# Normalizing three attention units right behind their softmax, and unread TensorE products in the opening rounds

## The chip, the cores and the metric

The kernel runs on one core of one Trainium2 chip. The time is device time in microseconds (us) of one execution, lower is better. Three runs gave 1222.81, 1223.53 and 1228.38 us; their median is 1223.53 us.

## The reference

Chunked attention over 4 x 8 heads and 768 positions, then two feed-forward blocks on its output, in float32:

```python
for c in range(nc):                       # chunks of 32 queries
    scores = scale * np.matmul(q_c, k_full.transpose(0, 1, 3, 2))   # 8 memory keys and up to 56 of context
    scores = scores - np.max(scores, axis=-1, keepdims=True)
    a = np.exp(scores)
    a = a / (np.sum(a, axis=-1, keepdims=True) + 1e-09)
    out[:, :, c_start:c_end] = np.matmul(a, v_full)
x = out.transpose(0, 2, 1, 3).reshape(B * S, H * D)                 # 3072 x 512
h = x @ w_in;  g = np.maximum(h, 0.0) + np.log1p(np.exp(-np.abs(h)));  x = g @ w_out
return (x @ w_a) * (x @ w_b) @ w_o2
```

## The kernel before

The 3072 rows of x are worked off in eight tiles of 384. Each large product is made of three float32r products of a high and a low part, so every weight matrix is split on the chip first. A `Weight` does that in two halves: `top` (ScalarE) and `value` (VectorE) first, then `high` (ScalarE) and `low` (VectorE).

Attention of the first tile goes through six `Block`s of 64 queries. They stand in rounds, a software pipeline written out by hand: round `i` normalizes block `i-2`, places block `i-4` into x, makes the scores of block `i`, transposes block `i-2` on TensorE (`pat`), multiplies with the values of block `i-3` (`pxb`), and converts one weight beside that. Ten rounds come before the first feed-forward product `ph0` of tile 0, which reads all of x of that tile.

Attention of later tiles goes through `Unit`s of 128 queries, laid between the products of the tile before. Tile 0 has 16 products `ph0` to `ph15` (`emit_h`), each followed on ScalarE by three activations `e` and a cast of `g` to its high part, on VectorE by `g` and its low part (`emit_soft`), and, two products later, by the second product (`emit_x1`, written `px`). In the same stretch the remaining 24 weights are converted, half by half (`convert`), and units 3, 4 and 5, which are the second tile, run through `EARLY_STEPS`: scores (`sc`), softmax (eight reductions on VectorE, eight exponentials on ScalarE), normalization on VectorE, eight transposes on TensorE (`pa`), copies of them (`af`), values (`pxa`), and a place into x.

In tile 0 the instructions of all five engines stand in the order in which the code issues them (a manual schedule), so each engine works through its own queue in that order and waits on semaphores for the others. Two PSUM banks carry the tag `att`: the two score banks of a unit, its two transposes and its values take them in turn, so that the second score bank of unit `u+1` is the bank of the values of unit `u` and is free when these have been placed. `acc`, with one bank a tag, holds the scores of a block, and `h`, with two, holds `ph`.

Of the kernel before, what the change touches and what calls it, by code (L numbers as in the profile page):

```python
# [9 lines left out]
F32 = mybir.dt.float32  # L10
# [11 lines left out]
         (3, "values"), (3.1, "place"))  # L22
START = 1.7
SETS = 1
EARLY_STEPS = (((4.9, "scores"), (5, "soft"), (6, "norm_v"), (9, "flip_p"), (10.9, "values"), (11, "place")),
               ((11.9, "scores"), (12, "soft"), (14, "norm_v"), (17, "flip_p"), (18.9, "values"), (19, "place")),
               ((19.9, "scores"), (20, "soft"), (22, "norm_v"), (25, "flip_p"), (26.9, "values"), (27, "place")))
EARLY = len(EARLY_STEPS)
NEXT_LATER = 1.5

# [2 lines left out]
EARLY_RAW = (2, 4, 5, 6, 7, 8)  # L33
PACKED_AT = (0, 0.1, 2, 2.1)
AHEAD = 6
ROUNDS_CV = 7
CV_DONE = 15
OUT_TAGS = "eegg"
# [7 lines left out]
def attn_moe_moe2(ctx: ExitStack, tc: tile.TileContext, q, k, v, mem_k, mem_v,  # L46
                  w_in, w_out, w_a, w_b, w_o2, out):
    nc = tc.nc
# [5 lines left out]
    P = 128  # L54
# [17 lines left out]
        name=nc.get_next_instruction_name(), act_func_set_id=6, ins=[], outs=[]))  # L72
# [8 lines left out]
    ps = ctx.enter_context(tc.tile_pool(name="ps", bufs=2, space=PSUM))  # L81
# [9 lines left out]
    def fetch(dst, key, src):  # L91

        u = n_w[0]
        n_w[0] += 1
        raw = wp.tile([P, 1024], U32, tag="w", name=f"raw{u}")
        nc.sync.dma_start(raw if len(src.shape) == 2 else raw.rearrange("p (a b) -> p a b", a=src.shape[1]),
                          src.bitcast(U32))
        dst[key] = u, raw
# [33 lines left out]
    def fetch1(n):  # L132
        dst, f = uses[n]
        if dst is w1:
            fetch(w1, f, w_in[:, f * P:(f + 1) * P].rearrange("(k p) f -> p k f", p=P))
        else:
            fetch(w1o, f, w_out[f * P:(f + 1) * P, :])

    masks = [ap.tile([P, KB], F32, name=f"mask{i}") for i in range(4)]
    ident = wp.tile([P, P], F32, tag="w", name="ident")  # L140
# [234 lines left out]
    def normalize(engine, sm, st):  # L375
        nc.vector.tensor_scalar(st[:, 2, :], st[:, 1, :], 1.0e-9, None, ALU.add)
        nc.vector.reciprocal(st[:, 3, :], st[:, 2, :])
        r = st[:, 3, :].rearrange("p (h o) -> p h o", o=1)
        engine.tensor_tensor(sm, sm, r.to_broadcast([P, sm.shape[1], KB]), ALU.mult)

    class Unit:
# [57 lines left out]
        def flip2(self):  # L439
            self.flip((2, 3))  # L440

        def norm_v(self):
            normalize(nc.vector, self.sm, self.st)

        def flip_p(self):
# [18 lines left out]
        def place(self):  # L464
# [3 lines left out]
            nc.scalar.copy(xh, self.px)  # L468
            nc.vector.tensor_tensor(xl, self.px, xh.bitcast(F32), ALU.subtract)  # L469

    blocks = [Block(u) for u in range(BPT)]
    units = [Unit(u) for u in range(B * NU)]

    plan = []
    for i, unit in enumerate(units[UPT:]):
        at = 2 * NF1 * (i + 1) // UPT - START + NEXT_LATER * (i == EARLY)
        steps = STEPS
        if i < EARLY:
            steps = EARLY_STEPS[i]
            at = steps[-1][0]  # L480
# [321 lines left out]
    def order():  # L802
# [6 lines left out]
        def fetch_to(n):  # L809
            nonlocal n_w1  # L810
            while n_w1 < min(n, len(uses)):
                fetch1(n_w1)
                n_w1 += 1
# [10 lines left out]
        packed[1].load(1)  # L824
        fetch_to(1 + ROUNDS_CV + AHEAD)
        weights = [Weight(*use) for use in uses]
# [4 lines left out]
            getattr(weights[0], step)()  # L831
        for i in range(BPT + 4):
            for d, step in ROUND:
                if d is None:
                    n = i if step == "low" else i + 1
                    if 0 < n <= ROUNDS_CV:
                        getattr(weights[n], step)()
                elif 0 <= i - d < BPT:
                    getattr(blocks[i - d], step)()

        rest = weights[1 + ROUNDS_CV:]
        firsts = [(w.top, w.value) for w in rest]
        seconds = [(w.high, w.low) for w in rest]
        halves = [firsts[0]]
        for x, y in zip(firsts[1:] + [()], seconds):
            halves += [x, y]
        n_half, n_point = [0], [0]

        def convert():

            n_point[0] += 1
            while n_half[0] * 3 * CV_DONE < n_point[0] * len(halves) and n_half[0] < len(halves):
                for step in halves[n_half[0]]:
                    step()
                n_half[0] += 1

        def att_at(slot):
            while plan and plan[-1][0] <= slot:
# [6 lines left out]
        for n, e in enumerate(pre[:n_pre]):  # L865
            t, i = divmod(n, PRE)
# [27 lines left out]
        for t in range(NTILE):  # L894
            if t == 1:
                early.close()
                early.enter_context(tc.manual_schedule(engines={mybir.EngineType.SP, engines["P"], engines["V"]}))
            if t == NTILE - 1:
                assert not plan
                actx.close()  # L900
                early.close()
                ctx.enter_context(tc.manual_schedule(engines={mybir.EngineType.SP, *engines.values()}))
                late["x"] = ctx.enter_context(tc.tile_pool(name="late", bufs=5))
            for f in range(NF1):
                ph = emit_h(t, f)
                if t == 0:
                    fetch_to(1 + ROUNDS_CV + AHEAD + len(rest) * (f + 1) // CV_DONE)
                    convert()
                    emit_soft(t, f, ph, nc.vector, convert)
                    convert()  # L910
                elif t < NTILE - 1:
                    emit_soft(t, f, ph)
                else:
                    emit_soft(t, f, ph, nc.vector, partial(slot, 2 * f), partial(slot, 2 * f + 1))
                att_at(2 * (NF1 * t + f))
                if len(pend) >= LAG:
                    emit_x1(*pend.pop(0))
                pend.append((t, f))
                att_at(2 * (NF1 * t + f) + 1)
# [48 lines left out]
        while jobs:  # L968
            if len(jobs) == 3 and pair_step.late:
                pair_step.late.pop()()  # L970
            next_job()

    order()


# [28 lines left out]
```

## Time and profile before

| | |
|---|---|
| median of three runs | 1223.53 us |
| profiled execution, its own time | 1221.9 us |
| its span in the trace | 1219.9 us |
| TensorE busy with matmuls | 1181.3 us (97%) |
| VectorE, ScalarE, GpSimd busy | 734.4, 537.8 and 277.9 us |
| mean granted TensorE clock | 0.986 of full |

The span runs from the first to the last instruction on the core. TensorE is called PE, its weight loads PEld, VectorE DVE, ScalarE ACT. [...] In the rows, "[2.84 <-DVE work L368]" means that the engine stood 2.84 us ahead of this instruction and that an instruction of line 368 on VectorE ended the wait.

### The profile page before, as it was taken

What the parts mean: (1) busy time and instruction counts of PE and PEld (TensorE: products, weight loads), DVE (VectorE), ACT (ScalarE), POOL (GpSimd) and SP (SyncE); (2) the same over time, 40 slices, a digit from 0 to 9 for tenths busy, and PEclk for the clock granted to TensorE, in tenths of its full rate; (3) what the DMA queues carried; (4) which work ended last, traced back from release to release, by engine and by line L of the source; (5) the groups of instructions that cost most, each with busy time, mean ns of one, the idle gap of its engine ahead of it and who ended that gap; (6) DMA issues with size and microseconds to landing.
All of it is one profiled execution on the core that took longest, in us unless ns stands there. A gap on an engine that the chain in (4) does not pass through costs nothing.

```text
span 1219.9 us, 21427 instructions
## 1 busy us (share of the span) xinstructions
PE 1181.3 (97%) x7920; PEld 1119.7 (92%) x7920; DVE 734.4 (60%) x1706; ACT 537.8 (44%) x1329; POOL 277.9 (23%) x249
## 2 busy tenths in 40 slices
PE   6888999999999999999999999999999999999998
PEld 6787999999989999999999999999999999999997
DVE  6778565555645546555357777764666456664565
ACT  5788755575655756556464433312012111212010
POOL 1000222233222222222242877500211002200000
PEclk7799999999999999999999999999999999999999
DMA  9943335344352343533164987679463975469521
GB/s 243 299 149 83 75 96 123 93 97 92 111 104 79 98 96 93 112 101 95 44 225 160 375 295 275 264 245 376 158 233 118 354 270 177 151 214 382 197 78 52
DMA packets 198696, 209.84 MB, mean 172 GB/s; under 512 B 121616, under 2 KB 149952, under 8 KB 198592
## 3 DMA queue, kind: packets, MB, share of 16 engines
q1 hardware_dynamic: 198208, 208.43, 53.6%
q8 instruction: 62, 1.02, 0.3%
q14 instruction: 42, 0.34, 0.1%
q0 software_dynamic: 384, 0.05, 0.0%
HBM read 158.11 MB, written 50.33 MB: 171 GB/s over the span
## 4 chain that ended last, share of the span: by engine, by line
PE 82%; DVE 5%; ACT 4%; SPq 4%; DMA 2%; issue 2%; DVEq 0%; ACTq 0%
PE ph L514 18%; PE py L724 16%; PE px L537 16%; PE pV L701 8%; PE pW L701 8%; PE pX L701 8%; PE pY L701 4%; SPq L176 1%; SPq L178 1%; ACT sm L372 1%; PE pxa L461 1%; PE sc L418 1%; DVE af L436 1%; ACT e L521 1%; ACT e L522 1%
## 5 line engine op out<-in xcount | busy, mean ns | idle before, releaser
L514 PE MATMUL ph<-x,w 128*128 128x384 f32 x1536 | 295.5, 340 | 9.0 <-DVE x L469 4.4
L514 PEld LDWEIGHTS ph<-x,w 128*128 128x128 f32 x1536 | 269.7, 190 | 13.7 <-DVE x L469 6.0
L724 PE MATMUL py<-w2o,c 128*128 128x512 f32 x864 | 223.1, 394 | 0.7 <-DVE c L794 0.5
L524 DVE SCALAR_TENSOR_TENSOR g<-ph,e 128x384 f32<-128x384 f32 x128 | 71.3, 557 | 222.9 <-ACT e L522 216.2
L724 PEld LDWEIGHTS py<-w2o,c 128*128 128x128 f32 x864 | 159.9, 188 | 27.0 <-DVE c L794 1.2
L783 ACT CAST c<-c 128x384 fp32r<-128x384 f32 x48 | 24.7, 514 | 303.9 <-DVE c L781 271.3
L701 PE MATMUL pX<-x,u 128*128 128x384 f32 x576 | 115.5, 334 | 0.0
L520 ACT ACTIVATE e<-ph 128x384 f32<-128x384 f32 x128 | 62.3, 487 | 118.9 <-PE ph L514 104.9
L733 DVE TENSOR_TENSOR y<-py,y 128x512 f32<-128x512 f32 x120 | 82.9, 691 | 48.6 <-PE py L724 48.1
L701 PEld LDWEIGHTS pX<-x,u 128*128 128x128 f32 x576 | 102.1, 188 | 4.1
L436 DVE STREAM_TRANSPOSE af<-sm 32x256 f32<-32x256 f32 x180 | 78.2, 434 | 2.5
L521 ACT ACTIVATE e<-e 128x384 f32<-128x384 f32 x128 | 67.3, 526 | 4.1
L522 ACT ACTIVATE e<-e 128x384 f32<-128x384 f32 x128 | 67.3, 526 | 3.9
L779 DVE TENSOR_TENSOR d<-pW,q 128x384 f32<-128x384 f32 x48 | 26.7, 557 | 68.3 <-PE pW L701 68.3
L372 ACT ACTIVATE sm<-sm,st 128x96 f32<-128x96 f32 x168 | 60.5, 362 | 7.5 <-DVE st L368 7.5
L793 ACT CAST c<-c 128x384 fp32r<-128x384 f32 x48 | 24.6, 513 | 78.1 <-DVE c L791 77.1
L701 PE MATMUL pW<-xs,u 128*128 128x384 f32 x288 | 57.8, 335 | 0.0
L701 PE MATMUL pV<-xx,u 128*128 128x384 f32 x288 | 57.8, 335 | 0.0
L701 PE MATMUL pV<-xs,u 128*128 128x384 f32 x288 | 57.6, 334 | 0.0
L701 PE MATMUL pW<-xx,u 128*128 128x384 f32 x288 | 57.6, 334 | 0.0
L701 PE MATMUL pY<-xs,u 128*128 128x384 f32 x288 | 57.6, 334 | 0.0
L701 PEld LDWEIGHTS pV<-xx,u 128*128 128x128 f32 x288 | 51.5, 188 | 4.1
(247 smaller groups left out, 2226.1 us busy)
## 6 DMA issues: line engine op xcount, KB each, us to landing
u<-u_scratch SPq DMA_DIRECT2D x108, 512.0 KB
u_scratch<-u SPq DMA_DIRECT2D x36, 512.0 KB
w2o<-w2o_scratch SPq DMA_DIRECT2D x36, 512.0 KB
u<-u_scratch SPq DMA_DIRECT2D x36, 256.0 KB
raw<-in_moe_w_in_dram SPq DMA_DIRECT2D x16, 512.0 KB
raw<-in_moe_w_out_dram SPq DMA_DIRECT2D x16, 512.0 KB
vn<-in_v_dram SPq DMA_DIRECT2D x35, 176.0 KB
raw_a<-in_moe_w_a_dram SPq DMA_DIRECT2D x12, 512.0 KB
```

Source lines behind the costliest of these rows:

```text
L372: nc.scalar.activation(sm[:, h], sm[:, h], AF.Exp, bias=st[:, 0, h:h + 1], scale=-1.0, accum_out=st[:, 1, h:h + 1])
L436: nc.vector.transpose(out=af[32 * kb:32 * kb + 32, x], in_=self.sm[32 * x:32 * x + 32, :, 32 * kb:32 * kb + 32])
L514: nc.tensor.matmul(ph, lhsT=a, rhs=c, start=n == 0, stop=n == 3 * KT - 1)
L520: nc.scalar.activation(e, ph, AF.Abs)
L521: nc.scalar.activation(e, e, AF.Exp, scale=-1.0)
L522: nc.scalar.activation(e, e, AF.Ln, bias=1.0)
L524: nc.vector.scalar_tensor_tensor(g, ph, 0.0, e, ALU.max, ALU.add)
L537: nc.tensor.matmul(acc[t][i][:, :TT], lhsT=a, rhs=c, start=f == 0 and m == 0, stop=f == NF1 - 1 and m == 2)
L701: nc.tensor.matmul(bank[:, :TT], lhsT=u[:, j, a, kt * P:kt * P + P], rhs=x[:, c, kt, :], start=first_ and m == 0, stop=m == 3 * KH - 1, sk ...
L724: nc.tensor.matmul(b, lhsT=c[:, x, r], rhs=w[:, y], start=n == 0, stop=n == 3 * GROUP - 1)
L733: tt(y, b, y, ALU.add)
L779: tt(d21, w[:, :TT], q, ALU.add)
```

## The change

Two things. First, for units 3, 4 and 5 the steps `soft` and `norm_v` become one step `weigh`: it takes the next half of a weight conversion from the common list, issues that half's ScalarE part, then the softmax, then the half's VectorE part, and at once the normalization on VectorE. The halves are taken from the same list, so as many are converted as before. Second, `FILL` names 16 places in the rounds, and `warm` issues there, 44 in all, products of the 128x128 identity with itself into a bank of tag `h` that nothing reads.

```diff
-EARLY_STEPS = (((4.9, "scores"), (5, "soft"), (6, "norm_v"), (9, "flip_p"), (10.9, "values"), (11, "place")),
-               ((11.9, "scores"), (12, "soft"), (14, "norm_v"), (17, "flip_p"), (18.9, "values"), (19, "place")),
-               ((19.9, "scores"), (20, "soft"), (22, "norm_v"), (25, "flip_p"), (26.9, "values"), (27, "place")))
+EARLY_STEPS = (((4.9, "scores"), (5, "weigh"), (9, "flip_p"), (10.9, "values"), (11, "place")),
+               ((11.9, "scores"), (12, "weigh"), (17, "flip_p"), (18.9, "values"), (19, "place")),
+               ((19.9, "scores"), (20, "weigh"), (25, "flip_p"), (26.9, "values"), (27, "place")))
...
+FILL = {(2, "scores"): 11, (2, "flip"): 14, (3, "flip"): 1, (3, "values"): 1, (4, "scores"): 2, (4, "flip"): 1,
+        (4, "values"): 1, (5, "scores"): 2, (5, "flip"): 1, (5, "values"): 1, (6, "flip"): 4, (6, "values"): 1,
+        (7, "flip"): 5, (7, "values"): 1, (8, "values"): 1, (9, "place"): 1}
...
+    halves, n_half = [], [0]
+
+    def next_half():
+        n_half[0] += 1
+        return halves[n_half[0] - 1]
...
-        def norm_v(self):
+        def weigh(self):
+            on_scalar, on_vector = next_half()
+            on_scalar()
+            self.soft()
+            on_vector()
             normalize(nc.vector, self.sm, self.st)
...
+    def warm(n):
+
+        if n:
+            n_fill[0] += 1
+            bank = ps.tile([P, 512], F32, tag="h", name=f"fill{n_fill[0]}")
+            for _ in range(n):
+                nc.tensor.matmul(bank[:, :P], lhsT=ident, rhs=ident, start=True, stop=True)
...
         for i in range(BPT + 4):
             for d, step in ROUND:
+                warm(FILL.get((i, step), 0))
```

On VectorE, behind the reductions of unit 3's softmax, the queue before (`w12` is the low half of a weight, `g0_3` the result for `ph3`, `tmp14` and `tmp15` first halves of weights, `st3` and `sm3` the sums and the weights of unit 3):

```order
L125 TENSOR_TENSOR w12_878<-tmp12_773,w12_878 128x512
L524 SCALAR_TENSOR_TENSOR g0_3_885<-ph0_3_861,e0_3_881 128x384
L116 TENSOR_SCALAR tmp14_888<-raw14_617 128x512
L117 SCALAR_TENSOR_TENSOR tmp14_888<-raw14_617,tmp14_888 128x512
L504 TENSOR_TENSOR g0_3l_892<-g0_3_885,g0_3h_891 128x384
L125 TENSOR_TENSOR w13_895<-tmp13_790,w13_895 128x512
L116 TENSOR_SCALAR tmp15_899<-raw15_693 128x512
L117 SCALAR_TENSOR_TENSOR tmp15_899<-raw15_693,tmp15_899 128x512
L376 TENSOR_SCALAR st3_844<-st3_844 128x8
L377 RECIPROCAL st3_844<-st3_844 128x8
L379 TENSOR_TENSOR sm3_843<-sm3_843,st3_844 128x768
L125 TENSOR_TENSOR w14_934<-tmp14_888,w14_934 128x512
```

The same place on VectorE in the changed kernel:

```order
L128 TENSOR_TENSOR w12_907<-tmp12_837,w12_907 128x512
L385 TENSOR_SCALAR st3_910<-st3_910 128x8
L386 RECIPROCAL st3_910<-st3_910 128x8
L388 TENSOR_TENSOR sm3_909<-sm3_909,st3_910 128x768
L546 SCALAR_TENSOR_TENSOR g0_3_952<-ph0_3_931,e0_3_948 128x384
L119 TENSOR_SCALAR tmp14_955<-raw14_681 128x512
L120 SCALAR_TENSOR_TENSOR tmp14_955<-raw14_681,tmp14_955 128x512
L526 TENSOR_TENSOR g0_3l_959<-g0_3_952,g0_3h_958 128x384
L128 TENSOR_TENSOR w13_962<-tmp13_854,w13_962 128x512
L119 TENSOR_SCALAR tmp15_966<-raw15_757 128x512
L120 SCALAR_TENSOR_TENSOR tmp15_966<-raw15_757,tmp15_966 128x512
L128 TENSOR_TENSOR w14_998<-tmp14_955,w14_998 128x512
```

The three instructions of the normalization have moved up past seven others, ahead of `g0_3`. On ScalarE at the same place, before (`raw13` is the first half of a weight, `sm3` the eight exponentials, `w12` the high half, `e0_3` the first activation for `ph3`):

```order
L111 ACTIVATE raw13_199<-raw13_199 128x512
L372 ACTIVATE sm3_843,st3_844<-sm3_843,st3_844 128x96 x8
L122 CAST w12_878<-tmp12_773 128x512
L520 ACTIVATE e0_3_881<-ph0_3_861 128x384
L521 ACTIVATE e0_3_881<-e0_3_881 128x384
```

And in the changed kernel:

```order
L114 ACTIVATE raw13_199<-raw13_199 128x512
L125 CAST w12_907<-tmp12_837 128x512
L381 ACTIVATE sm3_909,st3_910<-sm3_909,st3_910 128x96 x8
L542 ACTIVATE e0_3_948<-ph0_3_931 128x384
L543 ACTIVATE e0_3_948<-e0_3_948 128x384
```

The cast of `w12` now stands ahead of the exponentials. Units 4 and 5 are moved likewise; there the half is `raw20` and `w25`. On TensorE the last rounds and the first product read like this before (`pat4`, `pat5` transposes of blocks, `pxb` their values):

```order
L352 MATMUL pxb2_522<-afb2_469,vv2_159 64x64 x8
L344 MATMUL pat4_552<-ident_75,work4_439 96x128 x4
L352 MATMUL pxb3_558<-afb3_515,vv2_159 64x64 x8
L344 MATMUL pat5_576<-ident_75,work5_493 96x128 x4
L352 MATMUL pxb4_582<-afb4_551,vv4_168 64x64 x8
L352 MATMUL pxb5_593<-afb5_575,vv4_168 64x64 x8
L514 MATMUL ph0_0_604<-x0_435,w0_277 128x384 x12
```

And in the changed kernel:

```order
L361 MATMUL pxb2_567<-afb2_505,vv2_159 64x64 x8
L490 MATMUL fill11_596<-ident_75 128x128 x4
L353 MATMUL pat4_602<-ident_75,work4_473 96x128 x4
L490 MATMUL fill12_608<-ident_75 128x128
L361 MATMUL pxb3_610<-afb3_558,vv2_159 64x64 x8
L490 MATMUL fill13_627<-ident_75 128x128 x5
L353 MATMUL pat5_634<-ident_75,work5_534 96x128 x4
L490 MATMUL fill14_640<-ident_75 128x128
L361 MATMUL pxb4_642<-afb4_601,vv4_168 64x64 x8
L490 MATMUL fill15_653<-ident_75 128x128
L361 MATMUL pxb5_655<-afb5_633,vv4_168 64x64 x8
L490 MATMUL fill16_664<-ident_75 128x128
```

Nothing is moved on TensorE; the fills stand between. The largest, of 11 and 14, stand ahead of the scores of block 2 and of the transposes of block 0.

## Rows read from the trace of the kernel before

**Rows 1.** Windows: busy us (instructions) by engine, granted clock, DMA share, GB/s.
```profile
17.30:34.30 17.00, 13.87 (x160) 12.07 (x160) 14.81 (x68) 14.53 (x50) 0.00 (x0) 0.50 0.94 238
34.40:37.70 3.30, 1.67 (x32) 1.27 (x32) 3.06 (x14) 3.07 (x12) 0.00 (x0) 1.00 1.07 255
37.80:48.00 10.20, 7.28 (x58) 6.31 (x53) 6.46 (x16) 4.94 (x15) 0.00 (x0) 0.50 1.06 372
48.00:135.00 87.00, 78.45 (x758) 74.90 (x757) 65.50 (x163) 71.10 (x170) 0.00 (x0) 1.00 0.50 139
362.10:368.80 6.70, 6.10 (x19) 6.10 (x20) 1.02 (x2) 1.54 (x3) 0.00 (x0) 0.50 0.39 94
```
**Rows 2.** Timeline of TensorE in the rounds: start, us, instruction, [idle before].
```profile
18.29 0.56 PE L293 MATMUL scb<-kt,qt 64*64 64x88 f32 x4 [2.84 <-DVE work L368]
...
22.51 1.06 PE L344 MATMUL pat<-ident,work 128*96 128x128 f32 x4 [2.02 <-ACT raw L111]
...
40.65 1.06 PE L344 MATMUL pat<-ident,work 128*96 128x128 f32 x4 [2.45 <-ACT x L358]
41.64 1.98 PE L352 MATMUL pxb<-afb,vv 96*64 96x64 f32 x32
44.09 4.22 PE L514 MATMUL ph<-x,w 128*128 128x384 f32 x12 [0.47 <-ACT x L358]
```
**Rows 3.** Timeline of VectorE and ScalarE where the rounds end.
```profile
39.95 0.56 DVE L379 TENSOR_TENSOR work<-work 128x384 f32<-128x384 f32 x1
...
43.66 0.37 ACT L358 CAST x<-pxb 128x256 fp32r<-128x256 f32 x1 [0.48 <-PE pxb L352]
44.06 0.42 DVE L359 TENSOR_TENSOR x<-pxb,x 128x256 fp32r<-128x256 f32 x1 [0.43 <-ACT x L358]
```
**Rows 4.** Timeline of TensorE in tile 0, around the units.
```profile
73.88 1.05 PE L450 MATMUL pa<-ident,sm 128*96 128x128 f32 x8 [3.37 <-DVE sm L379]
74.69 2.36 PE L514 MATMUL ph<-x,w 128*128 128x384 f32 x12
...
82.42 0.40 PE L293 MATMUL sc<-kn,qn 64*64 64x88 f32 x8
...
97.17 1.05 PE L450 MATMUL pa<-ident,sm 128*96 128x128 f32 x8 [2.82 <-DVE sm L379]
...
120.37 1.05 PE L450 MATMUL pa<-ident,sm 128*96 128x128 f32 x8 [2.34 <-ACT raw L111]
```
**Rows 5.** Timeline of ScalarE around the exponentials of units 3 and 4.
```profile
63.37 0.38 ACT L372 ACTIVATE sm<-sm,st 128x96 f32<-128x96 f32 x1 [1.34 <-DVE st L368]
...
66.26 0.60 ACT L122 CAST w<-tmp 128x512 fp32r<-128x512 f32 x1
66.77 0.48 ACT L520 ACTIVATE e<-ph 128x384 f32<-128x384 f32 x1
...
82.53 0.49 ACT L520 ACTIVATE e<-ph 128x384 f32<-128x384 f32 x1 [0.91 <-PE ph L514]
...
87.14 0.38 ACT L372 ACTIVATE sm<-sm,st 128x96 f32<-128x96 f32 x1 [1.34 <-DVE st L368]
```
**Rows 6.** Timeline of VectorE behind the softmax of unit 3, to its place.
```profile
66.90 0.69 DVE L125 TENSOR_TENSOR w<-tmp,w 128x512 fp32r<-128x512 f32 x1 [2.32 <-ACT w L122]
68.40 0.56 DVE L524 SCALAR_TENSOR_TENSOR g<-ph,e 128x384 f32<-128x384 f32 x1 [0.81 <-ACT e L522]
...
72.33 0.17 DVE L376 TENSOR_SCALAR st<-st 128x8 f32<-128x8 f32 x1
...
72.77 0.96 DVE L379 TENSOR_TENSOR sm<-sm,st 128x768 f32<-128x768 f32 x1
73.65 0.69 DVE L125 TENSOR_TENSOR w<-tmp,w 128x512 fp32r<-128x512 f32 x1
74.25 0.55 DVE L524 SCALAR_TENSOR_TENSOR g<-ph,e 128x384 f32<-128x384 f32 x1
...
81.69 0.68 DVE L469 TENSOR_TENSOR x<-pxa,x 128x512 fp32r<-128x512 f32 x1
```

More of the change, by code (lines that the diff above doesn't have):

```diff
@@ L469, in place @@
             nc.vector.tensor_tensor(xl, self.px, xh.bitcast(F32), ALU.subtract)
+    def warm(n):
[4 more added lines that the diff above has]
+                nc.tensor.matmul(bank[:, :P], lhsT=ident, rhs=ident, start=True, stop=True)
+    n_fill = [0]
     blocks = [Block(u) for u in range(BPT)]
@@ L843, in order @@
         seconds = [(w.high, w.low) for w in rest]
[L844 to L847, printed above, removed]
+        halves.append(firsts[0])
+        for x, y in zip(firsts[1:] + [(lambda: None, lambda: None)], seconds):
+            halves.extend((x, y))
+        n_point = [0]
         def convert():
@@ L852, in convert @@
             while n_half[0] * 3 * CV_DONE < n_point[0] * len(halves) and n_half[0] < len(halves):
-                for step in halves[n_half[0]]:
+                for step in next_half():
                     step()
-                n_half[0] += 1
         def att_at(slot):
```

## The prediction

> **What bounds the kernel now.** I began with the page's shares: TensorE is busy 97% of the span, so only time in which it stands, or runs at half clock, can be won. The table by windows puts both ahead of 135 us. From 17.3 to 34.3 and from 37.8 to 48.0 the granted clock is 0.50, between them 1.00, and from 48 to 135 it is 1.00 while TensorE is busy 78.45 of 87 us [rows 1]. So I went to the timeline. In the rounds TensorE stands 2.84 us ahead of the scores of block 2, 2.02 ahead of the first transposes and 2.45 ahead of the last [rows 2]. In tile 0 it stands 3.37, 2.82 and 2.34 ahead of the transposes `pa` of units 3, 4 and 5, together 8.53, nearly all that is missing there [rows 4].
>
> The releasers say why. Ahead of `pa` it is the normalization of the unit, or the work on ScalarE beside it. The exponentials of unit 3 end at 66.26 [rows 5], yet its normalization starts at 72.33 on VectorE, behind seven instructions that it doesn't need, and TensorE, which had reached `pa` at 70.51, waits for it [rows 4, 6]. In the rounds VectorE is busy 14.81 and ScalarE 14.53 of 17 us, TensorE 13.87 at half clock, and 3.06 and 3.07 of 3.3 in the next stretch [rows 1]: the two smaller engines set the pace, and a faster TensorE there only waits longer. That ends with the last normalization, at 39.95 to 40.51 [rows 3]. From then on each step waits for the one before: transposes, their copy, values, place, `ph0`, three of these on TensorE at half clock [rows 2].
>
> **The moved normalization, unit 3.** ScalarE stands 1.34 us ahead of the exponentials for the reductions; the cast of `w12`, which cost 0.51 behind them (66.26 to 66.77), now lies in that gap [rows 5]. So `e3` and all behind it come 0.51 earlier. VectorE stands 2.32 us ahead of the low half of `w12`; that, about 0.60, now lies there too, since its cast is done [rows 6]. The normalization follows when the exponentials end, about 66.35, and takes 1.32 (72.33 to 73.65): done by 67.7. `g3` has its turn at 68.40 - 0.51 = 67.89 [rows 6]. So it fits ahead of `g3`, with 0.2 to spare, and is done 2.8 us before TensorE asks for it at 70.51. The stall of 3.37 goes.
>
> This adds a wait: the normalization stands at the head of VectorE's queue until the last exponential, and `g3`, and behind it TensorE's second product, wait with it. I cost that at nothing, because VectorE stood there before, 2.32 and 0.81 us [rows 6]. [...] The rows decide, since `g3` could not have run: its activations end after the normalization does.
>
> What is late next: the scores of unit 4 need the bank that holds the values of unit 3 until these are placed. `g4` comes at 67.89 + 3.93 (68.40 to 72.33) + 0.60 (73.65 to 74.25) = 72.42 instead of 74.25 [rows 6], so this chain wins 1.83 (0.51 and the 1.32 that no longer lie in it). The place at 81.69 ends at 80.54 instead of 82.37. TensorE, 3.37 earlier, reaches the scores at 82.42 - 3.37 = 79.05 [rows 4] and stands about 1.5. Its lead is then 1.83.
>
> **Units 4 and 5.** Ahead of `e6` ScalarE stood 0.91 us for `ph6` at 82.53 [rows 5]; `ph6` now comes 3.37 earlier, so that gap closes and the chain's lead is 1.83 + 0.91 = 2.74. Unit 4 adds its own 0.51 (ScalarE's gap is again 1.34 [rows 5]) and 1.32: 4.57. TensorE leads by 1.83 + 2.82 = 4.65 at `pa4` and gives 0.1 back at the scores of unit 5. Unit 5 has no scores behind it in tile 0, so its 2.34 counts whole: **6.9 us**. Bounds: 6.0 if ScalarE's 0.91 isn't won (2 x 1.83 + 2.34), 8.5 if nothing is given back.
>
> The halves come from the same list, so no conversion is added; VectorE and ScalarE, busy 65.50 and 71.10 of 87 us [rows 1], have room for the same work in 80. No transfer is added. Loads wait for TensorE's reads and shift with them; with the DMA share at 0.50 [rows 1] I cost that at nothing; if one were late, its wait would come out of the 6.9.
>
> **The fills.** The trace has no such product. Nearest are the eight transposes, full height and 128 columns: 73.88 to 74.69, 0.10 us each at full clock [rows 4]; four at half clock take 40.65 to 41.64, 0.25 each [rows 2]. A float32 product makes two passes (the 16 values products of two blocks count x32 [rows 2]). So a fill costs 0.20 at full clock and 0.50 at half. Below, 0.10 if its passes overlapped; above, two passes as long as those of `ph`, 2.36/12 and 4.22/12 [rows 2, 4]: 0.39 and 0.70. I take 0.20, as the transposes have its shape. Then 11 make 2.2 us in a gap of 2.84, and 14 make 2.8 in one of 2.02 plus the 1.0 or so that block 2's scores shorten by at full clock. They fit, if the clock holds; at 0.39 they'd overrun by 1.5 and 2.4. The other 19 (3.8 us) lie where TensorE waits for VectorE.
>
> What they can bring is the clock. It fell when TensorE stood 2.84 us at 15.45 and stayed at half through the rounds; later it didn't fall in a stand of 3.37 [rows 1, 2, 4]. So I can't read off that the fills hold it; that they fill just the gaps in which it fell makes it likelier than not. What it brings if held to `ph0`, by halves: transposes 1.06 to 0.53, values of block 5 0.99 to 0.50, `ph0` 4.22 to 2.36 [rows 2, 4]: 0.53 + 0.49 + 1.86 = 2.9. The place between them, 43.66 to 44.48 [rows 3], stays. I take off 0.2, for the fills between the last values and because the start of `ph0` waits for the place. **2.7 us**, from 0 (not held) to 2.9.
>
> **The sum.** 6.9 + 2.7 = 9.6 off the profiled execution's own 1221.9 gives 1212.3. The median is 1.6 above that execution; I carry this along: 1223.5 - 9.6 = **1213.9**.
>
> **The rivals.** *The clock falls again ahead of the end of the rounds.* It fell between 37.7 and 37.8, with TensorE busy only 1.67 of the 3.3 us before [rows 1]; the fills add about 1.0 there, which may not change that. Then only the units count: 1223.5 - 6.9 = 1216.6.
> *The stalls only move.* If the places of units 3 and 4 come no earlier, the scores behind them give 3.37 and 2.82 back, and 2.34 + 2.7 = 5.0 remains: 1218.5. For it: ScalarE's 71.10 of 87 leaves little air. Against it: the lead of `g4` is made of two terms that both have a row.
> *The fills hold TensorE up (slower).* At half clock 14 cost 7.0 against a stand of 2.02, 5.0 late at the first transposes; the 19 others cost 9.5 against stands of some 4.5 (3.3 - 1.67 and 10.2 - 7.28 [rows 1]). `ph0` comes 10.0 late, the units win 6.9: 1223.5 + 3.1 = 1226.6. It needs the clock to fall in spite of the first 11 and stay down; it decides once the delay passes 6.9. Against it: the clock did rise at 34.3 under steady work.
> *The clock elsewhere.* At 362.1 to 368.8 it was at half [rows 1]. 6.1 busy us at half clock are some 3 us lost; another execution may lack that stretch or have one more: 3 us either way, in the range.
>
> **How the numbers follow.** Forecast 0.52, clock falls again 0.23, stalls move 0.12, slower 0.04, 0.09 for what I haven't named. A measurement of this kernel can tell about 0.5%, 6.1 us, from no change. The forecast (two in a hundred aside), most of the second case and a few of the rest lie below 1217.4: faster 0.74; the third case and what is left of the second: same 0.23; slower 0.03. The range of 8 in 10 takes in the first three, and a lost or gained stretch of half clock around the first: 1209.5 to 1219.5.
>
> **What would show it.** Right: no stand ahead of `pa` of units 3 to 5; one of 1 to 2 us ahead of the scores of unit 4, ended by VectorE's place, and next to none at unit 5; the normalization straight behind the exponentials, `g` not later; granted clock 1.00 where it was 0.50 ahead of 48, and `ph0` in 2.4 us, ending near 45.5. Wrong: `ph0` again in 4.2 us, the first transposes later than 22.5, or stands at the scores of units 4 and 5 as long as those that left.

## The result: 1205.2 us, and the profile after

The changed kernel took 1205.17 us (median of 4 runs, 1204.67 to 1207.71) against 1224.42 for the kernel before beside it: a ratio of 0.984, 95% interval 0.981 to 0.987. It is faster, by about twice the 9.6 us that were forecast, and lies below the range. Its profiled execution took 1205.47 us, with a span of 1203.5 and a mean granted clock of 1.00 of full speed. Of all executions one, in e6, took 2315.53 us; it is left out of the median given there.

One count has to be set right first. The places in `FILL` add up to 48 fills, and the trace has 96 records of them; "44 in all" is wrong wherever it stands, and the small fills outside the two groups of 11 and 14 are 23, not 19.

The same windows as in [rows 1], in the kernel after (busy us and instructions of PE, PEld, DVE, ACT and POOL, then granted clock, DMA share, GB/s):

```profile
17.30:34.30 17.00, 15.77 (x232) 14.24 (x232) 15.67 (x64) 15.77 (x57) 0.00 (x0) 1.00 0.96 231
34.40:37.70 3.30, 2.76 (x32) 2.41 (x32) 3.09 (x15) 2.95 (x12) 0.00 (x0) 1.00 1.02 232
37.80:48.00 10.20, 9.45 (x116) 8.24 (x117) 6.62 (x14) 6.94 (x15) 0.00 (x0) 1.00 1.05 369
48.00:135.00 87.00, 85.38 (x788) 82.50 (x787) 69.74 (x185) 74.07 (x187) 4.17 (x6) 1.00 0.51 143
362.10:368.80 6.70, 6.70 (x41) 6.64 (x40) 3.94 (x10) 3.96 (x9) 3.50 (x3) 1.00 0.34 120
```

The clock is at full speed in every window, and in the fourth TensorE is busy 85.38 us instead of 78.45. The timeline of TensorE in the rounds answers [rows 2] (a fill leaves two records, so 22 are 11 fills):

```profile
14.32 2.72 PE L490 MATMUL fill<-ident 128*128 128x128 f32 x22
17.24 0.38 PE L302 MATMUL scb<-kt,qt 64*64 64x88 f32 x4 [0.20 <-DVE work L377]
...
18.42 3.39 PE L490 MATMUL fill<-ident 128*128 128x128 f32 x28
21.65 0.60 PE L353 MATMUL pat<-ident,work 128*96 128x128 f32 x4
...
34.65 0.61 PE L353 MATMUL pat<-ident,work 128*96 128x128 f32 x4 [1.28 <-ACT x L367]
...
38.47 0.61 PE L353 MATMUL pat<-ident,work 128*96 128x128 f32 x4 [1.06 <-ACT x L367]
...
41.43 2.66 PE L536 MATMUL ph<-x,w 128*128 128x384 f32 x12
```

The two long stands are gone, and `ph0` takes 2.66 us instead of 4.22; the stand ahead of the last transposes is 1.06 instead of 2.45. Fourteen fills take 3.23 us from the first to the transposes behind them (18.42 to 21.65): 0.23 a fill. The timeline of ScalarE and VectorE at unit 3 answers [rows 5, 6], that of TensorE [rows 4]:

```profile
59.17 0.38 ACT L381 ACTIVATE sm<-sm,st 128x96 f32<-128x96 f32 x1 [0.84 <-DVE st L377]
...
60.29 0.69 DVE L128 TENSOR_TENSOR w<-tmp,w 128x512 fp32r<-128x512 f32 x1
62.18 0.17 DVE L385 TENSOR_SCALAR st<-st 128x8 f32<-128x8 f32 x1 [1.20 <-ACT sm L381]
...
62.62 0.96 DVE L388 TENSOR_TENSOR sm<-sm,st 128x768 f32<-128x768 f32 x1
63.67 0.56 DVE L546 SCALAR_TENSOR_TENSOR g<-ph,e 128x384 f32<-128x384 f32 x1
...
66.14 1.03 PE L463 MATMUL pa<-ident,sm 128*96 128x128 f32 x8
...
76.38 0.41 PE L302 MATMUL sc<-kn,qn 64*64 64x88 f32 x8 [1.28 <-DVE x L482]
```

The low half of the conversion lies where VectorE waited, the normalization starts 0.03 us behind the last exponential (whose sum is read out until 62.15), `g3` follows at once, and `pa` waits for nothing. A stand of 1.28 is left ahead of the scores of unit 4, for the place.

So the two mechanisms can be seen. They don't make 19 us. The stage table shows where the rest is; I read it from the timelines, as the time from one first instruction to another: from the last normalization of the rounds to the first turn of the second tile; from there to tile 1; tiles 2 and 4 from their first `ph` to that of the next tile. The last column is explained under the experiments.

| kernel | rounds' end | rest of tile 0 | tile 2 | tile 4 | packets around the start of tile 4 |
|---|---|---|---|---|---|
| before | 8.49 | 86.80 | 75.1 | 80.69 | -43, 100 |
| after | 6.46 | 79.71 | 75.5 | 76.13 | 0, 113 |
| e0, before again | 8.63 | 88.44 | 75.1 | 79.93 | -43, 100 |
| e1, units alone | 8.10 | 80.47 | 75.3 | 80.27 | -42, 97 |
| e2, fills alone | 6.46 | 86.85 | 74.9 | 75.23 | 1, 114 |
| e3, two fills | 8.63 | 92.94 | 75.3 | 75.59 | -92, 57 |
| e4, after again | 6.46 | 80.47 | 76.7 | 75.34 | 0, 114 |
| e9, after + 40 records | 6.44 | 79.67 | 78.3 | 81.80 | -53, 102 |
| e10, units + 88 records | 8.61 | 80.53 | 74.9 | 75.14 | 16, 121 |
| e11, before + 88 records | 8.64 | 92.84 | 74.9 | 75.18 | 22, 121 |

Between the first and the last normalization of the rounds lie 18.14 us in all of them, at either clock.

### The profile page after: what moved, and what is told of

The parts are those of the page before. It is cut to its first block, busy times and chain, and to the rows that moved or that the text cites. A ratio compares the mean times of both kernels' runs of the same rounds, so it can differ in the third digit from the quotient of the medians.

```text
span 1203.5 us, 21617 instructions
## 1 busy us (share of the span) xinstructions
PE 1180.9 (98%) x8016; PEld 1120.5 (93%) x8016; DVE 734.5 (61%) x1706; ACT 538.0 (45%) x1329; POOL 278.1 (23%) x249
## 3 DMA queue, kind: packets, MB, share of 16 engines
q8 instruction: 63, 1.03, 0.4%
## 4 chain that ended last, share of the span: by engine, by line
PE 86%; DVE 4%; ACT 3%; SPq 2%; DMA 2%; issue 1%; DVEq 0%; ACTq 0%
PE ph L536 19%; PE px L559 18%; PE py L746 16%; PE pW L723 8%; PE pV L723 8%; PE pX L723 8%; PE pY L723 4%; PE pxa L474 1%; PE sc L427 1%; DMA raw<-in_moe_w_in_dram 1%; SPq L185 1%; SPq L187 1%; ACT sm L381 1%; DVE tmp L120 1%; DVE af L445 1%
## 5 line engine op out<-in xcount | busy, mean ns | idle before, releaser
L536 PE MATMUL ph<-x,w 128*128 128x384 f32 x1536 | 292.2, 337 | 7.6 <-ACT x L481 4.1
L536 PEld LDWEIGHTS ph<-x,w 128*128 128x128 f32 x1536 | 266.6, 188 | 12.4 <-DVE x L482 5.0
```

Source lines behind the costliest of these rows:

```text
L536: nc.tensor.matmul(ph, lhsT=a, rhs=c, start=n == 0, stop=n == 3 * KT - 1)
```

## Experiments

**The scatter of the kernel before.** Theory A was that the gain beyond the forecast is the clock's chance, theory B that every run of before loses time at half clock.

> The kernel before, unchanged, to see what its executions scatter by. Both theories: a ratio of 1.00. Theory A (the 9 us beyond the forecast are stretches at half clock that a run of the kernel before has by chance): mean granted clocks spread from 0.98 to 0.995 and the time follows them, half of each half-clock microsecond. Theory B (they are lost in every run): the clocks lie close together, at 0.985 or below.

It took 1223.24 us, ratio 0.999 (0.996 to 1.002). Over all runs of the kernel before in this study, 77 with different times, the time follows the mean granted clock: 0.977 to 0.990, and 1.02 us for each 0.001 (correlation -0.94). At 0.989, about what the two stretches in the rounds alone leave (27.3 us at half are 0.011 of the span), the line gives 1219.0; the median of the 77 is 1224.4. So the middle run of before loses some 5 us more to half clock elsewhere. The clocks spread and the time follows them, as theory A had it, but even the best runs don't come near full clock: for those 5 us and for the rounds theory B holds.

**Each half of the change alone.**

```diff
-FILL = {(2, "scores"): 11, (2, "flip"): 14, ...}
+FILL = {}
```

> The moved normalization of units 3 to 5 alone, no fills. Both theories: no stand ahead of the transposes of units 3 to 5, the lead that arises between the first product and the last stand is 7.0 us, about 1217.3 us against 1224.4. The granted clock is still 0.50 in most of the rounds. Theory A: the rest of the run as before. Theory B: mean clock below 0.99 in every run.

Measured 1214.93 us, 0.990 (0.987 to 0.993).

```diff
-EARLY_STEPS = (((4.9, "scores"), (5, "weigh"), (9, "flip_p"), ...
+EARLY_STEPS = (((4.9, "scores"), (5, "soft"), (6, "norm_v"), (9, "flip_p"), ...
```

> The 44 fills alone, normalization as before. Theory A (fills win only what lies between the last normalization of the rounds and the end of the first product, 2.0 us in the trace of the changed kernel, and chance gives the rest): about 1221.5 us, stands ahead of the unit transposes as before. Theory B (a clock kept full in the rounds is worth more, there or later in every run): about 1212 to 1214 us, mean clock 0.997 or more in every run.

Measured 1215.68 us, 0.991 (0.988 to 0.994), clocks 0.993 to 0.999. The fills alone win some 9 us, not 2: nearer to theory B, though 1.7 us above its range. In the table both halves do in their places what was forecast (rounds' end 8.49 to 6.46, rest of tile 0 86.80 to 80.47). But e2 also has tile 4 in 75.23 us, and e1 in 80.27. Nothing in the fills' place explains this.

On top of that, only the two large groups of fills:

```diff
-FILL = {(2, "scores"): 11, (2, "flip"): 14, (3, "flip"): 1, ...}
+FILL = {(2, "scores"): 11, (2, "flip"): 14}
```

> Only the two large fills, of 11 and 14, normalization as before. If the clock, once kept through the start of the rounds, stays up by the kernel's own work: as with all 44. If the small fills are needed: the clock falls again near 34 to 38 us, the first product takes 4.2 us, and the run is 2 to 3 us slower than with all 44.

Measured 1224.83 us, 0.998 (0.996 to 1.001): no gain. The table by windows of this run shows the clock falling later, and in tile 0, where the stands ahead of `pa` are 3.36, 2.82 and 2.84 us (3.37, 2.82 and 2.34 in the kernel before):

```profile
34.80:48.30 13.50, 10.42 (x80) 8.74 (x82) 8.22 (x25) 7.65 (x21) 0.00 (x0) 0.50 1.03 342
72.30:79.00 6.70, 5.58 (x21) 5.54 (x22) 5.24 (x9) 2.99 (x6) 0.00 (x0) 0.50 0.00 0
99.60:103.00 3.40, 3.40 (x15) 3.35 (x13) 3.26 (x6) 2.17 (x5) 0.00 (x0) 0.50 0.45 152
123.50:126.80 3.30, 2.61 (x11) 2.55 (x12) 3.20 (x7) 2.25 (x6) 0.00 (x0) 0.50 0.57 92
```

So the two large groups only put the fall off from 17 to 34.7 us; the 23 small fills carry the clock to `ph0`. And the stands of tile 0, in which the clock stayed up in the trace of before, can cost it: the rest of tile 0 takes 92.94 us here, 6.1 more. An execution of the kernel before can lose there what its profiled one kept: in e0 the clock falls at 118.4, in the stand ahead of `pa` of unit 5.

**The changed kernel again, and its parts.**

> The changed kernel again, unchanged, for the scatter of its clock and a second trace. In 34 executions of the kernel before, time follows the mean granted clock: about 1.03 us more for each 0.001 less, and none has a clock over 0.989. Theory C: what the forecast missed is half-clock time and stands at the starts of later tiles, which come with a kernel whose rounds run at half clock, and which the changed kernel is free of. Then all executions here have a clock of 0.996 or more and a time of 1204.5 to 1208.5, the stage of tile 4 takes 75.2 to 76.2 us again, and no stand over 1 us is ahead of the values products (pxa) of tiles 4 to 6. Theory D: the changed kernel's first trace was lucky, and a later loss of 3 to 5 us falls on it as on any other. Then about half of the executions here lie at 1207.5 to 1212, with clocks of 0.993 to 0.997, and the new trace has such a stand or a half-clock stretch in tiles 4 to 6.

Measured 1205.43 us, 0.985 (0.982 to 0.988), clocks 0.997 to 1.000, tile 4 in 75.34. Not luck: the late loss is absent from this kernel. That is theory C so far; whether the rounds' clock is the reason, e9 and e10 tell. Two stretches at half clock do occur, at 79.5 (behind the stand of 1.26 at unit 4) and at 202.4.

```diff
-            on_scalar, on_vector = next_half()
-            on_scalar()
             self.soft()
-            on_vector()
             normalize(nc.vector, self.sm, self.st)
```

> The changed kernel with its fills, but the normalization alone moved behind the softmax: no half of a conversion around it. By the prediction's terms the 0.51 us of the cast come back behind the exponentials, so the chain through the place wins 1.32 a unit instead of 1.83: TensorE's lead is 1.32 after unit 3 (a stand of about 2.0 ahead of the scores of unit 4 instead of 1.28), 3.55 after unit 4 (0.6 ahead of those of unit 5), 5.9 after unit 5. Tile 0 from the first turn of the second tile to tile 1 takes 80.7 us instead of 79.7, the whole 1206.2. Rival: the wrapped half is worth nothing, since the casts only change places: 79.7 and 1205.2. Other rival: without it the normalization ends after g wants VectorE, and the second products come late: 81.5 or more, 1207 or more.

Measured 1208.01 us (five executions), 0.987 (0.984 to 0.990). Slower than forecast for it, 2.6 us over e4: the stand at unit 4 grows only from 1.26 to 1.71 (forecast 2.0), but the clock then stays at half for 6.8 us instead of 3.4, and the rest of tile 0 takes 83.04. Not a clean measure of the 0.51 us term: the longer stand came with 3.4 us more at half clock. The time is also that of the second rival, but its late `g` isn't there: `g3` starts at 64.31, as its activations end, and no stand but the one at unit 4 is left in tile 0.

**A buffer for the late wait.** In e1 the trace shows where tile 4 loses time. Timeline around its third product, all engines:

```profile
365.49 3.07 SPq L566 DMA_DIRECT2D x_scratch<-xo  x4
...
369.67 0.49 ACT L540 ACTIVATE e<-ph 128x384 f32<-128x384 f32 x1 [4.12 <-DMA x_scratch<-xo]
...
371.31 0.56 DVE L544 SCALAR_TENSOR_TENSOR g<-ph,e 128x384 f32<-128x384 f32 x1 [3.77 <-ACT e L542]
...
379.17 0.69 PE L472 MATMUL pxa<-af,vn 96*64 96x64 f32 x16 [2.12 <-DVE af L443]
```

The store of the last tile's output lands late; `e`, which shares its buffers, waits 4.12 us; `g` and the `af` transposes behind it on VectorE come late; TensorE stands 2.12 us, and the clock falls at 380.1. An issue of a load of q had taken 1.23 us at 348.68, too. In the kernel after, `e` waits 1.93 there and TensorE doesn't stand ahead of `pxa`.

```diff
-        e = mp.tile([P, TT], F32, tag="e", name=f"e{t}_{f}")
+        e = mp.tile([P, TT], F32, tag="e", name=f"e{t}_{f}", bufs=3)
```

> The run with the units' part alone (no fills, 1214.9 us, clock 0.983 to 0.987), with a third buffer under the tag that the activations e share with the tile's output on its way to memory. In its trace, and in two of the kernel before, the activations of the third product of tile 4 wait about 4 us for that output's store, VectorE comes 2.3 us later, TensorE stands 1.0 to 2.1 us ahead of the values products, and the clock falls for 3.4 us. If that wait is the cause of the later loss (theory C's form of it): no stand over 1 us there, no half-clock stretch behind 100 us in the trace, 1210.5 to 1212.5, clock 0.988 to 0.990. If the late stand has another cause (the loads of k and q that land late, or the clock by itself): stands and clock as they were, 1213.5 to 1216.

Measured 1213.83 us, 0.992 (0.989 to 0.994): 1.1 us below e1, but no better by the ratio (0.990 there), so no gain is shown. The stand ahead of `pxa` shrinks to 0.94, one of 1.95 ahead of the tile's first products remains, the clock falls at 353.1, and tile 4 takes 80.27 as before. With a third buffer the loss only moves, so the buffer alone is not the cause (the edit stands at all three places that use the tag).

> The changed kernel with the same third buffer. It has hardly a stand left there (0.47 us at 524), so theory C gives 1203.5 to 1205 and clocks of 0.998 or more in every execution; theory D gives a gain of 1 to 2 us against the changed kernel alone, which then has late losses. If the third buffer only moves the wait to the store's queue: as the changed kernel alone.

Measured 1205.56 us, 0.985 (0.982 to 0.988): nothing won. The changed kernel itself took 1205.17, 1205.43 and 1205.29 us in three sets of runs, in which the kernel before had medians from 1223.05 to 1226.44; so I compare times of different sets with it directly.

**Instruction packets.** Late loads and stores led to the DMA queues. The page of the kernel after lists them (packets, MB, share):

```profile
q1 hardware_dynamic: 198208, 208.43, 54.2%
q8 instruction: 63, 1.03, 0.4%
```

A packet of q8 is 1.03 MB / 63 = 16 KB. TensorE has 8016 matmuls and as many weight loads; a packet comes after every 127 matmuls on average, so I take q8 to carry TensorE's instructions, a reading of its kind and these counts alone: no view names the engine that a packet is for.

TensorE itself is not seen held by them: behind 130 us every stand of it over 0.1 us in six traces (before, after, e1, e4, e9, e10) is ended by work of another engine. Issues on SP are longer beside them: of the issues of k, q and output stores between 130 and 560 us in these traces, 36 took over 0.85 us instead of the usual 0.47, and 34 of these had a packet's start between 1.5 us ahead of them and their end; of the 1188 shorter ones 48 had. And the packets fall near the same matmul of the program in every execution of a kernel (58 of 62 within 8 matmuls in before and e0); the table above counts them from the first `ph` of tile 4. Where one falls about 100 behind a tile's first `ph` (97 to 109), with one some 45 ahead (37 to 53), the tile takes 80 us, at tile 4 and elsewhere (in e3, at tile 5: -37 and 109, 79.66 us). All eight such tiles among tiles 1 to 6 of the 16 traces (one of them in e12) take 78.3 to 81.8; of the others, outside e12, only one takes more than 78 (tile 6 of e0, 78.29, with 3.4 us at half clock). The 48 fills are 96 matmuls ahead of all that, and move the packets.

This can be tested without touching the clock, by small products at the start, where TensorE waits 2.5 us for the first load:

```diff
+        bank = [ps.tile([P, 512], F32, tag="h", name=f"tiny{i}") for i in range(2)]
+        for i in range(20):
+            nc.tensor.matmul(bank[i % 2][:32, :1], lhsT=ident[:32, :32], rhs=ident[:32, :1], start=True, stop=True)
         for i in range(KT):
             packed[0].turn(i)
```

> The changed kernel and, ahead of its first product, where TensorE waits 2.5 us for the first load, 20 unread products of 32 rows and one column (40 matmul records). The traces so far show packets of 16 KB on the queue q8, of kind instruction, one after every 128 matmuls on average, always at the same matmul of the program; in kernels with no fill the first product of tile 4 comes 43 matmuls after one and 100 before the next, in kernels with 44 fills it falls on one (0 and 114), and an issue on SP that meets one takes 0.9 to 1.9 us instead of 0.5. Theory E: the 4 to 5 us that tile 4 takes less in the changed kernel come from where those packets fall, since the fills add 88 matmuls ahead. Then 40 more complete 128 and bring the old places back: packets 43 before and 100 behind the first product of tile 4, a stand over 1 us there, tile 4 in 79.5 to 81 us instead of 75.3 to 76.8, and 1208.5 to 1211 in all with the rounds still at full clock. Theory C (the rounds at full clock keep the later tiles free): 1204.5 to 1208.3, tile 4 in 75 to 77.

Measured 1212.97 us, 0.989 (0.987 to 0.992): 7.5 us slower than the changed kernel, by 20 products of which none is read and none delays the start (first turn at 4.94 us). Timeline of this run in tile 4, and its DMA queues from 370 to 372 us:

```profile
355.42 3.89 PE L536 MATMUL ph<-x,w 128*128 128x384 f32 x11 [1.76 <-DVE x L482]
...
369.22 2.09 SPq L568 DMA_DIRECT2D x_scratch<-xo  x4
...
373.62 0.49 ACT L542 ACTIVATE e<-ph 128x384 f32<-128x384 f32 x1 [4.35 <-DMA x_scratch<-xo]
...
383.12 0.69 PE L474 MATMUL pxa<-af,vn 96*64 96x64 f32 x16 [2.12 <-DVE af L445]
```
```profile
q1 hardware_dynamic: 439, 0.61, 84.4%
q8 instruction: 1, 0.02, 2.9%
```

The late store and the stand ahead of `pxa` are back, with the rounds at full clock; the clock falls at 354.6 here, in the stand ahead of the tile's first products. Theory E stands, and C's form of it falls. It is 2 us slower than E's range, and tile 2 accounts for that: it takes 78.31 us, and has packets at -42 and 97 of its first `ph`, the places that cost tile 4 its time. The forecast for this run reckoned with 88 records of fills, 128 with these 40. They are 96 and 136, so the old places came back only roughly.

> The run with the units' part alone (no fills, 1214.9 us, rounds at half clock) and 44 such small products at the start (88 matmuls, as many as the 44 fills). Theory E: packets at 0 and 114 of tile 4, tile 4 in 75.2 to 76.8 us instead of 80.3, 1209.5 to 1211.5 in all, though the rounds run at half clock. Theory C: tile 4 in 79.9 to 80.7, 1213.5 to 1216. If the small products hold the start up, the first turn comes later than 4.95 us, and that much is added to both.

Measured 1212.16 us, 0.989 (0.987 to 0.991), as theory E had it. Timelines of its start and of tile 4:

```profile
2.30 4.85 PE L850 MATMUL tiny<-ident 32*32 32x1 f32 x88 [2.30 <-POOL ident masks.py:199]
7.08 0.77 PE L283 MATMUL ptk<-ident,kp 100*64 100x100 f32 x6
...
366.44 2.09 SPq L566 DMA_DIRECT2D x_scratch<-xo  x4
...
368.44 0.49 ACT L540 ACTIVATE e<-ph 128x384 f32<-128x384 f32 x1 [1.95 <-DMA x_scratch<-xo]
```

The small products hold the start up by 2.1 us (7.08 against 4.95). Without that it is 1210.0, 4.9 below e1: `e` waits 1.95, no stand over 0.7 is left in tile 4, though the rounds run at half clock. Its 88 records are 8 fewer than those of the fills; the packets fall at 16 and 121 instead of 0 and 113.

> The kernel before with the same 44 small products at the start and nothing else. Theory E: tile 4 in 75.2 to 76.8 us instead of 79.9 to 80.7, 1217.5 to 1220 in all against 1223.5. Theory C: 1222 to 1225, tile 4 as before. Either way the rounds at half clock, and the stands ahead of the transposes pa of 3.4, 2.8 and 2.3 us unchanged.

Measured 1223.05 us, 0.997 (0.995 to 1.000); less the late start of 2.2 (first turn at 7.08 us against 4.91), 1220.9. Tile 4 is as forecast, 75.18. The total is not, because in this trace the clock falls at all three stands of tile 0 (3.37, 2.82 and 2.79 us), as in e3 (rest of tile 0 92.84). Among its twelve runs those with a clock of 0.989 or 0.990 take 1216.4 to 1218.6.

```diff
-                nc.sync.dma_start(x1d[t, :, i, :], o)
+                (nc.sync if t == NTILE - 1 else nc.gpsimd).dma_start(x1d[t, :, i, :], o)
```

> The units' part alone, with the stores of a tile's output issued by GpSimd instead of SP. Theory E says that the fourth store, which stands 100 matmuls into tile 4 with its issue held 0.8 us by such a packet, makes the 2.1 us stand ahead of the values products there. Off SP it isn't held: that stand goes, about 2 us and perhaps the half-clock stretch behind it (1.7) are won, 1211 to 1213. [...]

Measured 1226.67 us, 1.001 (0.999 to 1.003), 11.7 slower than e1 and far from the 1211 to 1213 expected, though an issue on GpSimd took 0.54 to 0.60 us (in the trace of before, for `mem_n`, 0.54 in the median), against 0.47 on SP. Tiles 2 to 6 take 77.2 to 80.3 us, with a stand of 1.3 or more ahead of `pxa` in each of tiles 2 to 6.

**A version beyond.** The stand of 1.28 us at unit 4, filled with as many products as were taken from the rounds:

```diff
+            if u == UPT + 1:
+                for _ in range(3):
+                    nc.tensor.matmul(self.sc[0], lhsT=ident, rhs=units[u - 1].sm[:, :KT], start=True, stop=True)
```

> The changed kernel with three unread products less in the rounds (10 and 12 instead of 11 and 14) and three more, 384 columns wide, written into the free first score bank of unit 4 ahead of its scores, where TensorE stands 1.28 us. The number of matmuls ahead of tile 1 is the same, so the instruction packets keep their places. If the clock's fall behind that stand costs what the traces show (tile 0 from the first turn of the second tile to tile 1 in 80.45 us with it, 79.71 without): no half-clock stretch near 80 us, no execution under 0.998, median 0.5 to 1.5 us below the changed kernel beside it. Rival: the fall is the chip's choice whatever is done there, or three less in the rounds bring a fall back: no better than the changed kernel, or 1 to 3 us slower.

> The changed kernel, unchanged, as the partner of the run beside it: 1204.5 to 1208.3 us, clock 0.997 to 1.000, packets at 0 and 114 matmuls of tile 4.

e13 took 1205.60 us, 0.985 (0.981 to 0.988), e14 beside it 1205.29, 0.984 (0.980 to 0.988). No half-clock stretch is left at 80 us in e13, but its clocks, 0.997 to 1.000, are those of e14 (0.996 to 1.000), whose trace has none there either: the clock falls near 201 us in both. Nothing is won, and since the partner had no fall at 80 us to lose, the run can't tell what one costs.

## Why the prediction was right in its place and wrong in its sum

*The moved normalization, 6.9 us.* Right. The rest of tile 0 goes from 86.80 to 79.71: 7.1 (the same from e2 to the kernel after). The stalls ahead of `pa` are gone; the stand ahead of the scores of unit 4 is 1.28 (forecast about 1.5), at unit 5 0.34 (0.1); `pa` comes 2.6 us behind the end of the normalization (2.8). The waiting normalization cost nothing: `g3` starts 2.47 us ahead of `pa`, and 19.65 us behind the second tile's first turn instead of 20.17. `g3` could not have run earlier: its activations end at 63.64, the normalization at 63.58.

*The fills, 2.7 us.* Right in the mechanism, a little large. The clock held, the fills fitted (0.23 us each for 0.20), and the rounds kept their 18.14 us, VectorE and ScalarE now at 15.67 and 15.77 of 17. The prediction's "two passes" are two records a product in the trace (96 for the 48 fills); more the rows don't show. In the place where the gain was forecast it is 8.49 - 6.46 = 2.0; `ph0` gave 1.56 of 1.86.

*The rivals.* The clock didn't fall ahead of `ph0`, the stalls didn't only move, the fills held nothing up. With 23 small fills instead of 19 these cost 4.6 us at full clock instead of 3.8, and 11.5 at half instead of 9.5; the last rival's time would be 1228.6 instead of 1226.6, still outside the range.

*The step that failed* is the sum's silence on all that lies behind tile 0, and *the clock elsewhere*, which I took as chance, 3 us either way. I counted the matmuls that the fills add by their time on TensorE alone. Their number also moves every later instruction packet, and that is worth 4 to 5 us in tile 4 (80.69 and 79.93 before, 76.13, 75.34 and 75.23 in three traces after), shown in both directions by e9 and e10. That 96 records put the packets in a harmless place is luck: with 136 (e9) the kernel loses 7.5 us. I had looked at 362.1 to 368.8 in [rows 1], seen the clock, and not asked what TensorE waited for ahead of it. The trace of before answers:

```profile
356.81 1.37 SPq L178 DMA_DIRECT2D qn<-in_q_dram  x1
...
360.44 0.71 DVE L399 STREAM_TRANSPOSE kt<-kn 128x512 f32<-128x512 f32 x1 [1.69 <-DMA qn<-in_q_dram]
...
362.70 3.89 PE L514 MATMUL ph<-x,w 128*128 128x384 f32 x11 [1.96 <-DVE x L469]
```

A packet starts at 356.4. The issue of a load of q beside it took 1.37 us, VectorE stood 1.69 for such a load, its place into x came late, and TensorE stood 1.96, in which the clock fell. In the kernel after no packet falls among these loads' issues: VectorE stands 0.98, TensorE 1.25, and the clock stays up.

Second, half clock elsewhere is no symmetric chance: the middle run of before loses some 5 us by it and the changed kernel hardly any. In part it falls in stands that the change removes (unit 5 in e0, all three units in e3 and e11, which keep them), in part behind the packets.

Between the two profiled executions, 16.4 us: units 7.1, rounds' end 2.0, tile 4 4.6, tiles 6 and 7 together 1.0; 2.1 are the time from the first turn to the first normalization, 16.68 before and 14.61 after. It was 14.5 to 15.8 in the other 14 traces, fills or not, so I count that as chance. These make 16.8; tile 2 gives 0.4 back. The median of before lies another 2.5 above its profiled execution, by its clock.

The gain depends on both parts of the change in an odd way: the units with neither 1214.9 (e1), with moved packets alone 1210.0 (e10 less its late start), with the rounds' clock alone 1213.0 (e9, packets moved back, and to a costly place in tile 2 as well), with both 1205.2.

*Open.* Why a packet makes a load or store late; the runs move the packets by the number of matmuls ahead, so a packet's own part isn't separated from that number. In e1 the fourth store's issue was longer (four took 3.07 instead of 2.08); in e9 no issue was (2.09), and the stores landed 2.4 us late all the same. Moving the issue to another engine cost more than it could show.

## What to carry to other kernels

Count added instructions in two currencies, the engine's time and the place of everything behind them: a few dozen unread products can shift instruction packets into or out of a tight wait hundreds of microseconds later (20 of them in e9, 7.5 us lost some 200 to 350 us behind), so compare stage by stage to the end of the program before a gain is put down to the edit. Where time follows the mean granted clock over many runs, as here with 1.02 us for each 0.001, take the line's slope and the clock's distribution into the forecast instead of a symmetric chance. And give a stretch at half clock its cause: look for the stand ahead of it, and for what was late.

## What the hardware showed unexpectedly

- Twenty unread products of one column at the start of the program made it 7.5 us slower (e9, 1212.97 against 1205.4), as instruction packets came to lie at -42 and 97 of tile 2 and at -53 and 102 of tile 4, 200 to 350 us later.
- Stands as short as 1.3 us can be followed by 3.4 us at half clock (e4, at 79.5), and stands of 3.37 may not be [rows 4]; nearly the same stands cost some 6 us by the clock in e3 and e11.
- Two large groups of fills put the clock's fall off from 17.3 to 34.7 us and no further (e3); with the small ones, 0.23 us each, behind them it didn't fall in the rounds in any of eight traces.
